# Two transformer layers with a kept KV cache: 12 kept chunks instead of 11, joined chain steps, and V loads in halves

## The chip, the cores and the metric

The kernel runs on one core of a Trainium2 chip. The metric is device time in microseconds (us) of one execution. TensorE (PE in the profile) multiplies matrices, VectorE (DVE) and ScalarE (ACT) do elementwise work, GpSimd (POOL) one power, and SyncE (SP) issues nearly all loads from HBM into the on-chip memory. 16 DMA engines carry the loads.

## What is computed

One token of each of 8 sequences goes through block A (attention over a KV cache), block B (two small matrix products with gelu, a mixer and an MLP), then A and B again with the same weights and the same cache:

```python
def _A_ref(x, k_cache, v_cache, wq, wo):      # k_cache, v_cache: (8, 8, 4096, 256)
    q = (x @ wq).reshape(B, Sq, 16, 256).transpose(0, 2, 1, 3)
    k = jnp.repeat(k_cache, 2, axis=1); v = jnp.repeat(v_cache, 2, axis=1)
    p = softmax(jnp.einsum("bhqd,bhkd->bhqk", q, k) * 256 ** -0.5)
    o = jnp.einsum("bhqk,bhkd->bhqd", p, v)
    return o.transpose(0, 2, 1, 3).reshape(B, Sq, 16 * 256) @ wo

x = A_x
x = x + _A_ref(_layernorm(x), A_k_cache, A_v_cache, A_wq, A_wo)
x = x + _B_ref(_layernorm(x), B_w1, B_w2, B_w3, B_w4)
x = x + _A_ref(_layernorm(x), A_k_cache, A_v_cache, A_wq, A_wo)
x = x + _B_ref(_layernorm(x), B_w1, B_w2, B_w3, B_w4)
```

With a sequence length of 1 the mixer's shifts (pad and cut) give zeros, so of block B the kernel computes `x + gelu(layernorm(x) @ w3) @ w4`. All is bf16. The two caches are 268 MB together, and both passes need all of them.

## The kernel before

**Chunks and places.** For a sequence b, the 8 KV heads are four pairs (gp 0 to 3). K and V of a pair are four chunks each, of 1024 KB: 128 partitions by 16 rows of 256. On-chip memory has 15 places of one chunk (`NC`, L61; `slots`, L78). A chunk goes into a place, is used once, and hands the place back. A K chunk is transposed in its place by DVE (`transpose_k`, L755; L760), and its scores are taken by PE (`scores`, L762; L775), for most units by pairs of chunks; then ACT takes the exponentials (L784). A V chunk is multiplied with the transposed weights of the softmax (`pv`, L820; L828): 16 products of one row of 256 each, the first eight on the chunk's first half.

**Two passes, kept chunks.** The first pass (ps 0) of sequence b loads everything. The 11 chunks of `kept` (L64 and L65: K of pairs 3 and 2, V 1 to 3 of pair 3) stay in their places until the second pass (ps 1) of the same b has used them; there they are not loaded, and K of them is already transposed. One more chunk (`inner`, V 1 of pair 2) is moved to PSUM and back (`away` and `back`, L792 and L799: four DVE transposes each); it comes back into the place of kept K0 of pair 3, which is therefore not handed to the loads. A quarter of another (`part`) waits in PSUM also, so that 768 KB of it are loaded in the second pass. With 11 places kept, 4 are left for what streams.

**The chain.** Between the two passes of b lies work that depends on itself from end to end: `chain` (L494) takes the rest of the attention's output, the product with wo (L365), norm (L235 and POOL's power, L254), w3 (L383), gelu, w4 (L365), norm again, the projection with wq (L316), and spreading q (`give_q`, L904; `spread_q`, L328). It is a generator: each `yield` ends a step, and `step` (L885) takes the next step of each kind of generator ("chain", "last", "rest"). A `yield 2` makes the next call skip, so that POOL's power has time.

**The order.** All uses stand in one list, `items` (L551 to L604). `first_kept` puts the second pass's units that are not kept, and units of a later sequence, around the kept blocks; the V chunks of these units (16 in six of the eight cases, 8 in the last two) are put off until the chain. The first `AFTER` = 12 of them (L553) are in the set `narrow`: in the middle of each of their products (after the eighth) and at the end a step is taken. During them "last" steps wait (`alone`, L883, L889). What is left over (`due`) goes one by one between the K chunks of the next kept block (`block`, L555): K0 V K1 V K2 V K3 V. If the chain isn't done when its q is wanted, L955 and L956 take steps until it is. This is the order on PE; an engine takes its instructions in order.

**The loads.** `emit_loads` (L707) runs after each item. It issues on SP, in the order of use, as many loads as there are places handed back, each waiting on the chip for the last reader of its place. Two K chunks go as one load of 2048 KB where two neighbouring places come free (`both_for`, L677; issued at L722). Others are issued at L747. The last load of all goes in two halves (L750).

Of the kernel before, what the change touches and what calls it, by code (L numbers as in the profile page):

```python
# [17 lines left out]
def kernel(  # L18
# [43 lines left out]
    NP = 4  # L62

    kept = [(gp, 0, n) for gp in (GP - 1, GP - 2) for n in range(4)]  # L64
    kept += [(GP - 1, 1, n) for n in range(1, 4)]  # L65
    inner = (GP - 2, 1, 1)
    part = (GP - 1, 1, 0)
    Q4 = 4 * Dh
# [141 lines left out]
    def norm(x, nb, twice):  # L210

        def room(name, shape, at):
            n = shape[0] * shape[1]
            if nb < Bn:
                t = chn.tile([128, n * MID], FP32, tag=name)
                ap = t[:, 0 : n * nb]
            else:
                ap = scratch(at, n * nb)  # L220
            return ap.rearrange("p (s f b) -> p s f b", s=shape[0], f=shape[1])

        def bc(ap):
            return ap.unsqueeze(1).to_broadcast([128, 4, nb])

        xx = room("xx", (2, 4), 0)
        nc.vector.tensor_mul(xx[:, 0], x, wv[:].unsqueeze(2).to_broadcast([128, 4, nb]))
        nc.vector.tensor_mul(xx[:, 1], xx[:, 0], x)
        xs = room("xs", (1, 2), 512)[:, 0]
        nc.vector.tensor_reduce(  # L230
            xs, xx.rearrange("p s f b -> p s b f"), mybir.AxisListType.X, ALU.add
        )
        yield
        st = room_ps("st", nb).rearrange("p (s b) -> p s b", b=nb)
        nc.tensor.matmul(st, ones, xs, start=True, stop=True)  # L235
        yield
        mv = room("mv", (1, 2), 528)[:, 0]
        nc.vector.tensor_copy(mv, st)
        var = room("var", (1, 1), 608)[:, 0, 0]
        if nb == 1:  # L240
            nc.vector.scalar_tensor_tensor(
                var, mv[:, 0], mv[:, 0], mv[:, 1], ALU.mult, ALU.subtract, reverse1=True
            )
        else:
            nc.vector.tensor_mul(var, mv[:, 0], mv[:, 0])
            nc.vector.tensor_sub(var, mv[:, 1], var)


        ve = room("ve", (1, 2), 544)[:, 0]
        n = 2 if twice else 1  # L250
        rs = room("rs", (1, 2), 560)[:, 0]

        def power(k0, k1):
            nc.gpsimd.tensor_tensor(  # L254
                rs[:, k0:k1].rearrange("p n b -> p (n b)"),
                ve[:, k0:k1].rearrange("p n b -> p (n b)"),
                nhalf[:].to_broadcast([128, (k1 - k0) * nb]),
                ALU.pow,
            )

        if twice and nb == 1:
            nc.vector.scalar_tensor_tensor(
                ve[:, :, 0], var.to_broadcast([128, 2]), 0.0, eps2[:], ALU.max, ALU.add
            )
            power(0, 2)
        else:
            if twice:
                nc.vector.tensor_scalar(
                    ve[:, 1], var, 0.0, EPS * EPS / (1 + EPS), ALU.max, ALU.add
                )  # L270
                power(1, 2)
            nc.vector.tensor_scalar(ve[:, 0], var, 0.0, EPS, ALU.max, ALU.add)
            power(0, 1)
        xc = room("xc", (1, 4), 576)[:, 0]
        nc.vector.tensor_tensor(xc, x, bc(mv[:, 0]), ALU.subtract)  # L275
        yield 2
        if nb > 1:
            yield
        c = (1 + EPS) ** -0.5 if twice else 1.0
        rl = rs[:, n - 1]  # L280
        parts = ((0, 128, 0, 0, 3, 0), (0, 64, 64, 3, 4, 4), (64, 128, 64, 3, 4, 3))
        if nb == 1:
            nc.vector.scalar_tensor_tensor(
                xbs(1)[:, 0:4, 0], xc[:, :, 0], rl, low[:, int(twice)], ALU.mult, ALU.mult
            )
            parts = parts[1:2]
        for p0, p1, x0, f0, f1, to in parts:
            pp = slice(x0, x0 + p1 - p0)
            dst = xbs(nb)[p0:p1, to : to + f1 - f0, :]
            if nb == 1:  # L290
                nc.vector.tensor_scalar(dst, xc[pp, f0:f1], rl[pp], c, ALU.mult, ALU.mult)
            else:
                nc.vector.scalar_tensor_tensor(
                    dst,
                    xc[pp, f0:f1],
                    c,
                    rl[pp].unsqueeze(1).to_broadcast([p1 - p0, f1 - f0, nb]),
                    ALU.mult,
                    ALU.mult,
                )  # L300
        if twice and nb == 1:
            nc.vector.scalar_tensor_tensor(x, xc, rs[:, 0], x, ALU.mult, ALU.add)
        elif twice:
            nc.vector.tensor_tensor(xc, xc, bc(rs[:, 0]), ALU.mult)
            nc.vector.tensor_add(x, x, xc)
        yield

    def project_q(b0, nb, qT):

        yield from norm(xT[:, :, b0 : b0 + nb], nb, False)  # L310
        q_ps = room_ps("q", nb).rearrange("p (c b) -> p c b", b=nb)
        for j in range(2):
            for h in range(Hq):
                for fc in range(4):
                    w, xi = wblk(wq_sb, HD, 2 * h + j, fc)
                    nc.tensor.matmul(  # L316
                        q_ps[:, j * Hq + h, :],
                        w,
                        xbs(nb)[:, xi, :],
                        start=(fc == 0),  # L320
                        stop=(fc == 3),
                    )
                if h % 8 == 7:
                    yield
        nc.vector.tensor_copy(qT, q_ps)  # L325
        yield

# [27 lines left out]
    def add_cols(y_ps, rhs, w, rows, every, open=None):  # L355

        for fc in range(4):
            at = min(128 * fc, D - 128)
            for i in rows:
                if open is None:  # L360
                    start, stop = i == rows[0], i == rows[-1]
                else:
                    start = open[0] and fc == 0 and i == rows[0]
                    stop = open[1] and i == rows[-1]
                nc.tensor.matmul(  # L365
                    y_ps[:, fc, :],
                    w[:, i, at : at + 128],
                    rhs(i),
                    start=start,
                    stop=stop,  # L370
                    skip_group_check=open is not None,
                )
            if fc % every == every - 1 or fc == 3:
                yield

    def mlp_hidden(b0, nb):

# [2 lines left out]
        for c in range(HC):  # L380
# [7 lines left out]
                    stop=(fc == 3),  # L388
                )
            if c % 7 == 6:  # L390
                yield
        g_t = chn.tile([128, 2, HC * MID], FP32, tag="g")
        hh, g0 = g_t[:, 0, 0 : HC * nb], g_t[:, 1, 0 : HC * nb]
        if nb == 1:
# [6 lines left out]
        nc.vector.scalar_tensor_tensor(g0, hh, 2 * 0.044715, h_ps, ALU.mult, ALU.mult)  # L401
        nc.vector.scalar_tensor_tensor(g0, g0, 1.0, h_ps, ALU.add, ALU.mult)
        nc.scalar.activation(g0, g0, ACT.Tanh, scale=0.7978845608028654)
        yield
        nc.vector.scalar_tensor_tensor(
            HT,
            g0.rearrange("p (c b) -> p c b", b=nb),
# [12 lines left out]
    def z_cols(zall, gps):  # L420
# [14 lines left out]
        yield  # L435
        z_ps = misc[:, 384 : 384 + 4 * np_].rearrange("p (n g) -> p n g", n=4)
        nc.tensor.matmul(z_ps, ones, zm[:], start=True, stop=True)  # L437
        yield
        rz = chn.tile([128, 4, np_], FP32, tag=f"rz{np_}")
        nc.vector.reciprocal(rz[:], z_ps)  # L440
        return rz
# [9 lines left out]
    def half(o_ps, zall, g8, OT, ready):  # L451
# [20 lines left out]
        for j in range(2):  # L472
            nc.tensor.matmul(  # L473
                ot_ps[:, j], o_sb[:].rearrange("p (i j) -> p j i", j=2)[:, j], R[:], start=True, stop=True
            )
        yield
        nc.vector.tensor_copy(OT, ot_ps)
        locked.pop()
        yield
# [69 lines left out]
        ahead.append(units)  # L549

    tasks, items, due = [], [], []  # L551
    number, narrow = {}, set()
    AFTER = 12  # L553

    def block(k, v=None):  # L555

        fresh = [(number[v], 1, c) for c in range(4)] if v else []
        if k is None:
            due.extend(fresh)
            items.extend(due)  # L560
            due.clear()
            return
        number[k] = len(tasks)
        tasks.append(k)
        for c in range(4):
            items.append((number[k], 0, c))
            items.extend(due[:1])
            del due[:1]
            if c == 0:
                due.extend(fresh)  # L570

    def first_kept(b, units, before):
# [13 lines left out]
        for u in units:  # L586
            due.extend((number[u], 1, c) for c in range(4))
        narrow.update(due[:AFTER])
        items.extend(due[:AFTER])
        del due[:AFTER]  # L590

# [115 lines left out]
    def emit_loads(most=None):  # L707
        n = 0
        while loads and places and n != most:
# [32 lines left out]
                src = rows.rearrange("(a p y) d -> a p (y d)", a=4, y=16)[c]  # L742
            else:
                src = rows.rearrange("(p x y) d -> x p (y d)", x=4, y=16)[c]
            if loads:
                z0 = Q4 if tasks[t][0] == 1 and halfway(it) else 0
                nc.sync.dma_start(dst[:, z0:], src[:, z0:])  # L747
            else:
# [133 lines left out]

    alone = []  # L883

    def step(idx, calm=False):  # L885

        for kind in ("chain", "last", "rest"):
            e = next((e for e in gens if e["kind"] == kind), None)
            if e is None or (kind == "last" and alone and not e.get("locks") and idx < len(items)):  # L889
                continue  # L890
# [3 lines left out]
            if not e["of"] or e["n"] < e["of"] * (idx - e["at"] + 1) / max(e["until"] - e["at"], 1):  # L894
                e["n"] += 1
                had = len(locked)
                got = next(e["g"], gens)
                if len(locked) != had:
                    e["locks"] = len(locked) > had
                e["skip"] = 1 if got == 2 else 0  # L900
# [33 lines left out]
    for idx, it in enumerate(items):  # L934
# [17 lines left out]
        if kv == 0:  # L952
            if (ps, b) not in state:
                if ps == 1:
                    while (1, b) not in state:  # L955
                        step(10 * len(items))  # L956
                else:
                    state[0, b] = {}
            st = state[ps, b]
# [182 lines left out]
```

## Time and profile before

| what | us |
|---|---|
| median of 3 runs (1120.81 to 1122.77) | 1121.21 |
| the profiled execution, time | 1120.6 |
| the profiled execution, span from first to last instruction | 1118.8 |
| PE busy | 650.1 |
| DVE busy | 603.8 |
| ACT busy | 162.7 |

HBM read is 444.67 MB, 397 GB/s over the span; SP's hardware queue holds the 16 DMA engines for 95.9% of it. The page's chain of work that ended last has 52% on DMA, 23% on PE and 18% on DVE. No engine is busy for much more than half of the span. The page cuts the span into 40 slices of 28 us; its rows give the busy tenths of each engine in each slice, the clock granted to TensorE and the rate of the DMA engines. In a line of the timeline or of the groups, L828 is a line of the kernel, and the part after `<-` in brackets is what ended the engine's idle time. In the answers by window, each engine has its busy time and number of instructions, and the last three columns are the granted clock, the share of DMA engines busy, and GB/s. PE's clock was granted at 0.50 in most of the stretches beside the chain.

### The profile page before, as it was taken

The numbers are of one execution on the slowest core, as the hardware profiler recorded it, in microseconds if no ns is written. First come the engines' busy times: TensorE is split into PE (matmuls) and PEld (weight loads), VectorE is DVE, ScalarE is ACT, GpSimd is POOL, SyncE is SP. The second block draws the span as 40 slices with busy tenths as digits, with TensorE's granted clock in tenths as the row PEclk, the third lists the DMA queues.
The fourth block names the chain that finished last, engine by engine and source line by source line (L and its number), as shares of the span: only waits on it lengthen the run. The fifth ranks groups of instructions, "written<-read, shape, count | busy, mean of one in ns | idle before, by whom it ended". The sixth has DMA issues, their size and how long they took to land.

```text
span 1118.8 us, 29781 instructions
## 1 busy us (share of the span) xinstructions
PE 650.1 (58%) x13364; PEld 409.6 (37%) x13364; DVE 603.8 (54%) x1242; ACT 162.7 (15%) x610; POOL 16.4 (1%) x27
## 2 busy tenths in 40 slices
PE   3244467644775446844567446764467546766775
PEld 2122234422453224522345223442244324543555
DVE  4348732587227861478415783259722771585272
ACT  0011111211111110211102111121111111111020
POOL 0000000000000000000000000000000000000000
PEclk9999975855556555655556555575555765555565
DMA  9999999999989999999999999899998999799794
GB/s 360 396 424 428 421 416 383 420 427 421 409 359 425 423 423 411 365 427 427 418 409 373 427 425 417 357 419 423 423 420 356 425 422 418 306 429 416 313 406 199
DMA packets 55808, 446.59 MB, mean 399 GB/s; under 512 B 5881, under 2 KB 9857, under 8 KB 11649
## 3 DMA queue, kind: packets, MB, share of 16 engines
q1 hardware_dynamic: 55488, 444.32, 95.9%
q8 instruction: 104, 1.70, 0.6%
q10 hardware_dynamic: 192, 0.38, 0.1%
q14 instruction: 24, 0.19, 0.0%
HBM read 444.67 MB, written 0.01 MB: 397 GB/s over the span
## 4 chain that ended last, share of the span: by engine, by line
DMA 52%; PE 23%; DVE 18%; SPq 3%; issue 2%; ACT 1%; POOL 0%; DVEq 0%; ACTq 0%
DMA places<-in_A_v_cache_dram 27%; DMA places<-in_A_k_cache_dram 23%; DVE places L760 12%; PE sc L775 9%; PE o L828 7%; PE misc L316 3%; PE misc L365 3%; SPq L174 2%; DVE qbd L339 1%; DVE store L795 1%; DVE places L802 1%; SPq L747 1%; PE misc L473 1%; ACT p_n L784 1%; DMA wq_sb<-in_A_wq_dram 1%
## 5 line engine op out<-in xcount | busy, mean ns | idle before, releaser
L760 DVE STREAM_TRANSPOSE places<-places 128x512 uint32<-128x512 uint32 (+1 forms) x576 | 457.6, 854 | 97.0 <-DMA places<-in_A_k_cache_dram 93.8
L775 PE MATMUL sc<-places,qbd 128*8 128x256 bf16 (+1 forms) x4992 | 248.4, 351 | 230.3 <-DVE places L760 208.9
L828 PE MATMUL o<-places,ptw 128*8 128x256 bf16 x3968 | 241.3, 380 | 175.3 <-DMA places<-in_A_v_cache_dram 149.5
L775 PEld LDWEIGHTS <-qbd 128*8 128x8 bf16 x4992 | 129.1, 104 | 306.5 <-DVE places L760 158.5
L828 PEld LDWEIGHTS <-ptw 128*8 128x8 bf16 x3968 | 102.7, 102 | 246.8 <-issue 158.2
L784 ACT ACTIVATE p_n<-sc 128x256 bf16<-128x256 f32 x128 | 95.2, 744 | 344.2 <-PE sc L775 344.2
L930 ACT COPY ptw<-psv 128x32 bf16<-128x32 bf16 x248 | 50.7, 225 | 213.7 <-PE o L828 212.8
L818 ACT CAST psv<-misc 128x128 bf16<-128x128 f32 x64 | 17.0, 266 | 274.1 <-PE misc L811 274.1
L468 DVE MEMSET o<- 128x256 f32 x31 | 8.4, 272 | 68.6 <-ACT o_sb L467 37.1
L365 PEld LDWEIGHTS <-wo_sb 128*128 128x128 bf16 x1280 | 37.5, 102 | 17.2 <-issue 17.1
L316 PEld LDWEIGHTS <-wq_sb 128*128 128x128 bf16 x1152 | 34.3, 105 | 24.5 <-issue 14.1
L316 PE MATMUL misc<-xb,wq_sb 128*128 128x1 bf16 x1024 | 32.1, 165 | 3.6 <-DVE rz L440 2.3
L784 ACT ACTIVATION_READ_ACCUMULATOR p_n<-sc 128x1 f32 x128 | 33.7, 263 | 0.0
L365 PE MATMUL misc<-OT,wo_sb 128*128 128x1 bf16 x1024 | 30.6, 165 | 3.2 <-issue 2.3
L473 PE MATMUL misc<-R,o_sb 128*128 128x8 f32 x124 | 28.0, 336 | 7.1 <-ACT o_sb L467 7.1
L473 PEld LDWEIGHTS misc<-R,o_sb 128*128 128x128 f32 x124 | 25.3, 283 | 18.9 <-ACT o_sb L467 14.0
L325 DVE CAST qT<-misc 128x32 bf16<-128x32 f32 x8 | 1.5, 192 | 53.4 <-PE misc L316 53.4
L254 POOL TENSOR_TENSOR t<-t,nhalf 128x2 f32<-128x2 f32 (+2 forms) x20 | 14.0, 704 | 1090.1 <-DVE t L275 1090.1
L339 DVE CAST qbd<-misc 32x64 bf16<-32x64 f32 x92 | 19.8, 215 | 18.3 <-PE misc L335 17.3
L440 DVE RECIPROCAL rz<-misc 128x8 f32<-128x8 f32 (+1 forms) x33 | 6.5, 197 | 39.7 <-PE misc L437 21.3
L437 PE MATMUL misc<-zm,one 128*128 128x8 f32 (+1 forms) x66 | 17.7, 341 | 17.3 <-DVE zm L429 9.9
L437 PEld LDWEIGHTS misc<-zm,one 128*128 128x128 f32 x66 | 14.8, 277 | 27.0 <-DVE zm L429 12.4
(104 smaller groups left out, 305.4 us busy)
## 6 DMA issues: line engine op xcount, KB each, us to landing
places<-in_A_v_cache_dram SPq DMA_DIRECT2D x215, 1024.0 KB, 10.9
places<-in_A_k_cache_dram SPq DMA_DIRECT2D x66, 2048.0 KB, 22.9
places<-in_A_k_cache_dram SPq DMA_DIRECT2D x60, 1024.0 KB, 12.5
places<-in_A_v_cache_dram SPq DMA_DIRECT2D x8, 768.0 KB, 4.3
wo_sb<-in_A_wo_dram SPq DMA_DIRECT2D x1, 3584.0 KB
wq_sb<-in_A_wq_dram SPq DMA_DIRECT2D x3, 1024.0 KB
w_sb<-in_B_w_dram SPq DMA_DIRECT2D x1, 1568.0 KB
w_sb<-in_B_w_dram SPq DMA_DIRECT2D x3, 448.0 KB, 11.5
```

Source lines behind the costliest of these rows:

```text
L174: nc.sync.dma_start(t[:, fc * cols : (fc + 1) * cols], src[fc * 128 : fc * 128 + 128, :])
L316: nc.tensor.matmul(q_ps[:, j * Hq + h, :], w, xbs(nb)[:, xi, :], start=(fc == 0), stop=(fc == 3),)
L339: nc.vector.tensor_copy(qbd[32 * a : 32 * a + 32, :, :, a, :], qs.rearrange("p e (f g u h) -> p (e f) u g h", f=2, u=2, h=2)[:, :, u],)
L365: nc.tensor.matmul(y_ps[:, fc, :], w[:, i, at : at + 128], rhs(i), start=start, stop=stop, skip_group_check=open is not None,)
L437: nc.tensor.matmul(z_ps, ones, zm[:], start=True, stop=True)
L473: nc.tensor.matmul(ot_ps[:, j], o_sb[:].rearrange("p (i j) -> p j i", j=2)[:, j], R[:], start=True, stop=True)
L760: nc.vector.transpose(w, w)
L775: nc.tensor.matmul(sc[32 * k : 32 * k + 8, 128 * x : 128 * (x + nx)], qbd[:, ep, gp].rearrange("p a h -> p (a h)"), v, start=(n == 0), sto ...
L784: nc.scalar.activation(p_sb[:, :, :, 2 * u : 2 * u + 2].rearrange("p t i x -> p x t i"), sc[:, 256 * u : 256 * u + 256].rearrange("p (x t ...
L818: nc.scalar.copy(p_to, pt_ps.rearrange("p t k (a h) -> p a (t k) h", a=4))
L828: nc.tensor.matmul(o_ps[32 * q : 32 * q + 8, :], ptz[:, at : at + 8], v[:, y * Dh : (y + 1) * Dh], start=False, stop=(y >= 12), skip_group ...
L930: nc.scalar.copy(ptw[:, ring_of[it], :, 6:8], psv[slot_of[it[0]]][:, it[2]])
```

## The change

Seven things change together:

1. V 2 of pair 2 is kept as well: 12 kept chunks, three places for the stream.
2. `AFTER` is 10 instead of 12.
3. Eight yields of the chain become `yield 0` (and in `norm` the `yield 2` moves to its end). In a narrow item (`calm`), `step` goes on through them: two or three old steps become one.
4. In the kept blocks of the second pass the order is K0 K1 V V K2 K3 V V, instead of a V after each K. The first K of a pair scores both chunks, so both places are handed back ahead of the V.
5. The first 12 of the V chunks put off to the chain (all 8 where there are 8) are in the set `halved`: each goes as two loads of 512 KB, by rows 0 to 7 and 8 to 15.
6. Where the chain isn't done when its q is wanted, only chain steps are taken, through the `yield 0`.
7. V of a kept block, made due at its K1, comes after that.

```diff
     kept = [(gp, 0, n) for gp in (GP - 1, GP - 2) for n in range(4)]
-    kept += [(GP - 1, 1, n) for n in range(1, 4)]
+    kept += [(GP - 1, 1, n) for n in range(1, 4)] + [(GP - 2, 1, 2)]
...
         nc.tensor.matmul(st, ones, xs, start=True, stop=True)
-        yield
+        yield 0
...
         nc.vector.tensor_tensor(xc, x, bc(mv[:, 0]), ALU.subtract)
-        yield 2
+        yield 0
         if nb > 1:
             yield
...
             nc.vector.tensor_add(x, x, xc)
-        yield
+        yield 2
...
                 if h % 8 == 7:
-                    yield
+                    yield 0 if j == 1 and h == Hq - 1 else None
...
             if fc % every == every - 1 or fc == 3:
-                yield
+                yield 0 if fc == 3 else None
...
             if c % 7 == 6:
-                yield
+                yield 0 if c == HC - 1 else None
...
         nc.scalar.activation(g0, g0, ACT.Tanh, scale=0.7978845608028654)
-        yield
+        yield 0
...
-    number, narrow = {}, set()
-    AFTER = 12
+    number, narrow, halved = {}, set(), set()
+    AFTER = 10
...
+        two = k[0] == 1 and k[2] in keep
         for c in range(4):
             items.append((number[k], 0, c))
-            items.extend(due[:1])
-            del due[:1]
-            if c == 0:
+            if two and c % 2 == 0:
+                continue
+            items.extend(due[: 1 + two])
+            del due[: 1 + two]
+            if c <= two:
                 due.extend(fresh)
...
         narrow.update(due[:AFTER])
+        halved.update(due[: AFTER + 2])
...
-            if loads:
+            if loads and it not in halved:
                 z0 = Q4 if tasks[t][0] == 1 and halfway(it) else 0
                 nc.sync.dma_start(dst[:, z0:], src[:, z0:])
             else:
...
-    def step(idx, calm=False):
+    def step(idx, calm=False, kinds=("chain", "last", "rest")):
 
-        for kind in ("chain", "last", "rest"):
+        for kind in kinds:
...
                 got = next(e["g"], gens)
+                while calm and got == 0:
+                    got = next(e["g"], gens)
...
                     while (1, b) not in state:
-                        step(10 * len(items))
+                        step(10 * len(items), True, ("chain",))
```

The two other places where a `yield` becomes `yield 0` are in `z_cols` (after the product) and in `half` (after the products with R).

More of the change, by code (lines that the diff above doesn't have):

```diff
@@ L437, in z_cols @@
         nc.tensor.matmul(z_ps, ones, zm[:], start=True, stop=True)
-        yield
+        yield 0
         rz = chn.tile([128, 4, np_], FP32, tag=f"rz{np_}")
@@ L475, in half @@
             )
-        yield
+        yield 0
         nc.vector.tensor_copy(OT, ot_ps)
```

## The prediction

> **What bounds the kernel now.** I read the page first: the rate of the transfers by slice, and the issues.
>
> ```profile
> span 1118.8 us, 29781 instructions
> ...
> GB/s 360 396 424 428 421 416 383 420 427 421 409 359 425 423 423 411 365 427 427 418 409 373 427 425 417 357 419 423 423 420 356 425 422 418 306 429 416 313 406 199
> ...
> places<-in_A_v_cache_dram SPq DMA_DIRECT2D x215, 1024.0 KB, 10.9
> places<-in_A_k_cache_dram SPq DMA_DIRECT2D x66, 2048.0 KB, 22.9
> places<-in_A_k_cache_dram SPq DMA_DIRECT2D x60, 1024.0 KB, 12.5
> ```
>
> The reader sees transfers at 420 to 428 GB/s with a dent about every 133 us, and that nearly all loads are places of 1024 KB or pairs of them. Then I asked for windows: a long stretch between two dents, and 30 us around the ends of four of the eight chains (2, 4, 6 and 7, counted from 0). The last two columns are the share of the DMA engines and GB/s.
>
> ```profile
> 340.00:436.00 96.00, 49.07 (x922) 28.42 (x919) 62.32 (x107) 13.93 (x53) 0.70 (x1) 0.55 1.01 424
> ...
> 439.00:469.00 30.00, 23.46 (x507) 15.89 (x500) 7.92 (x32) 4.89 (x19) 0.55 (x1) 0.56 0.90 360
> ...
> 706.00:736.00 30.00, 23.45 (x512) 16.11 (x513) 7.93 (x32) 4.90 (x19) 0.55 (x1) 0.56 0.90 357
> ...
> 942.00:972.00 30.00, 20.77 (x476) 14.83 (x475) 12.84 (x39) 3.74 (x14) 0.67 (x2) 0.50 0.79 312
> 1036.00:1066.00 30.00, 20.77 (x442) 14.71 (x443) 10.44 (x42) 2.83 (x10) 1.25 (x2) 0.50 0.78 309
> ```
>
> A window loses 30 x (1 - rate/424): 3.0 us for chain 0 (176:206, 382 GB/s), 4.2 to 4.7 for chains 1 to 5, 7.9 and 8.1 for 6 and 7, 41 us in all. All else runs at the full 424, so time is bytes plus these dents. The timeline of chain 4 shows why a dent comes:
>
> ```profile
> 712.72 0.60 PE L828 MATMUL o<-places,ptw 128*8 128x256 bf16 x8 [1.48 <-DMA places<-in_A_v_cache_dram]
> ...
> 717.67 1.01 PE L316 MATMUL misc<-xb,wq_sb 128*128 128x1 bf16 x32
> ...
> 718.96 0.27 PE L335 MATMUL misc<-qT,identb 128*32 128x32 bf16 x4 [0.28 <-DVE qT L325]
> ...
> 720.22 0.60 PE L437 MATMUL misc<-zm,one 128*128 128x8 f32 x2 [0.99 <-DVE qbd L339]
> ...
> 720.75 1.02 PE L775 MATMUL sc<-places,qbd 128*8 128x256 bf16 x16
> ```
>
> Until 712.7 PE waits for V, so the transfers set the pace. Then the projections make PE late, the chain ends at 720, behind its last V, and the transpose back into K0's place (L802, 2.5 us) delays z. SP issues at 717.78 and next at 724.90; 721:726 moves 198 GB/s.
>
> **Bytes.** One V chunk fewer in each of 8 batches: 8 x 1.0486 MB / 424 GB/s = 8 x 2.47 = **-19.8 us**. All are in the dense stream, so nothing else hides them.
>
> **Halves.** 12 V chunks in six chains and 8 in two, 88 in all, go as 176 DMAs of 512 KB. In the trace's packet records the median is 311 ns at 8192 B (35613 packets) and 160 at 4096 B (384): 9 ns more per 8 KB. A chunk has 128 / 16 = 8 such packets on each DMA engine, so 72 ns; x 88 = **+6.3 us**, uncovered because the transfers are the bound. SP's 88 more issues of 0.33 us lie in waits. A lone 1 MiB load took 4.19 us from issue to landing (issued at 591.46 into an empty queue), while with four in flight the stream keeps 410 to 424 GB/s: the time above 2.47 shows only where the queue runs empty. The Trainium skill's "DMA: Bandwidth & Descriptors" (Anatomy of one DMA; Measured) speaks against halves: it gives each DMA a fixed 2.0 us and wants 1 MiB or more at a time. If each added DMA paid that in line, the change would lose 88 x 2.0 = 176 us, an estimate from that page that the queue of four here contradicts.
>
> **Closer steps, 10 narrow chunks, one place fewer.** A `yield 0` no longer ends a call of `step` in the narrow stretch. I counted the yields: from R (L473) to q's spreading the old chain takes 26 calls, two of them skipped, and a narrow V gives two calls, so 12 V end it two calls short. The new chain takes 16 (two skipped) and ends in the 8th V. PE work for these 8, from chain 4's rows at the granted 0.50: products with V 16 x 0.52 = 8.3; chain: R (L473) 0.64, wo 2.02, norm sums 0.59, w3 1.81, w4 1.81, norm sums 0.59, wq 4 x 1.01, spreading 0.27, in all 11.8. The joined steps put more of DVE's time before the next matmul: norm 2.0 us (L235's end at 693.35 to L291's at 695.35) less two half products, 1.0, twice; gelu 1.07 - 0.52; the sums before the norm 0.79 - 0.52, twice: 3.1 us. Together 23.2 us, 2.9 a chunk against 2.54 for its transfer: PE falls 2.9 us behind, and gains it back in chunks 9 and 10 (1.04 us each). Three places last 3 x 2.54 = 7.6 us; a half needs 4.19 - 1.24 = 2.95 to land, 0.52 of PE and 0.1 of SP, which leaves 4.0 us: 2.9 fits, barely. (Behind a waiting matmul of the chain the next half product is queued on PE, and behind that SP's next load.) With whole chunks it would leave 7.6 - 5.3 = 2.3, and it wouldn't fit.
>
> After the narrow stretch, K0 and K1 come at once: about 2.3 us of PE until K1's place is free (K0's takes the inner chunk), then two V, then two places. z still waits for L802's 2.5 us, but three or four transfers are then in flight. Beside the halves' cost I leave the dent of chains 0 to 5, 4.2 on average, at 2.2 us: 25 us at the 410 GB/s that 696:706 runs at (0.8), and K1's place 2.3 us late with two chunks queued (1.4, estimated from 726:731, where 366 GB/s cost 0.7 in 5 us, over 10 us). The edges are 0.5 (always enough in flight) and 6 (the dent stays and PE's lag costs 1.5). Six times -2.0 is **-12 us**.
>
> Chains 6 and 7 have only 8 V. Scoring began at 962.28, after a first narrow product at 933.74; now 933.74 + 23.2 + 1.0 = 958, 4 us earlier, also because the forced steps leave out the other half's z (waits 1.14 and 0.32 us, matmuls 1.5). One place fewer is 2.47 us less loaded ahead: 2 x -1.5 = **-3 us** (edges -6 and +2 each).
>
> **One place fewer elsewhere.** Issued less moved, in chunks: 2.6 at 675, 2.8 at 682, where K waits for DVE's transposes and scoring; now one less. 1.6 is still more than the 0.75 at which the flow broke (724). I take 0.5 us a batch, the size of the ripple now: **+4 us**; edges 0 and 36.
>
> Sum: -19.8 + 6.3 - 12 - 3 + 4 = -24.5. The profiled execution took 1120.6 (span 1118.8 and 1.8 around it), 0.6 under the median of the runs, 1121.2: 1096.1, or **1097** as a run's median. Startup (0 to 60 us) and the tail after the last V (1105.7) stay.
>
> **Rivals.**
> 1. The dents vanish (0.15). 41 us shrink to about 1 a chain, 8: -19.8 + 6.3 - 33 + 4 = -42.5, **1079**. For it: PE starts the kept blocks early. Against it: 2.9 of 4.0 us of slack is used at clock 0.50, which 716:721 kept with PE busy for 3.73 of 5 us; 731:736, busy for 4.52, reached 0.84. The Trainium skill's "TensorE: Matmul & The Clock Gate" (What's actually happening) has the clock go to full after about 3.4 us of busy time; by that rule, if denser steps count as busy, PE's 20 us of matmuls in the stretch would halve and the lag be gone.
> 2. The dents stay (0.20): the gap only moves from the forced steps to PE's waits for DVE, or halves come free together. -19.8 + 6.3 + 4 = -9.5, **1112**.
> 3. Slower (0.12): pairs of K need two neighbouring places, and SP takes loads in order. With a place fewer, a pair before the chain waits until the one before is transposed and scored, 4.8 + 2.0 us of DVE and PE, against 1.6 chunks (3.9 us) in flight: 2.9 us dry, in up to two pairs a batch. With that twice in most batches, 5 us x 8 = 40 instead of 4: 1097 + 36 = **1133**. It decides from 3.6 us a batch. For it: SP already waits 45.5 us for scoring at the pairs (L722). Against it: the loads ahead of use still count 6 there, by the order of items, against 7.
>
> The saving of bytes cannot fail to be there: the list of loads is fixed by `kept`.
>
> **Chances.** Forecast 0.53, rivals 0.15, 0.20, 0.12. Range 1078 to 1118: it holds the forecast, rival 2 and half of rival 1. Within 0.2% (2.2 us, about what a measurement can tell from no change) needs rival 3 at just its threshold: 0.02. Faster 0.87, slower 0.11.
>
> **What will show it.** The page should have V as x119 of 1024 KB, x8 of 768 and x178 of 512. HBM read falls by 8.4 MB. Steps right: 30 us windows at chains 1 to 5 at 375 GB/s or more, against 360; PE's projections (L316) done before the last narrow V; K scored directly behind. Wrong: rates under 400 in the 20 us before a chain (rival 3), or a window of 200 GB/s behind it (rival 2).

## The result, and the profile after

The changed kernel takes 1105.8 us (median of 4 runs, 1102.1 to 1111.0) against 1122.0: ratio 0.986, 95% interval 0.982 to 0.990. The forecast was 1097: the time fell by 16 us where 25 were forecast. The changed kernel's runs spread over 9 us, those of before over 3.

| | before | after |
|---|---|---|
| profiled execution, time, us | 1120.6 | 1105.07 |
| span, us | 1118.8 | 1103.2 |
| HBM read, MB | 444.67 | 436.28 |
| rate over the span, GB/s | 397 | 395 |

These are lines of the page after. In the changed kernel the code below `block` has moved down: the loads stand at L726 (pairs), L751 (whole) and L754 (halves), the transposes of K at L764, the scores at L779, the way back of the inner chunk at L806, the products with V at L832.

```profile
span 1103.2 us, 30150 instructions
...
GB/s 361 395 424 427 422 389 347 427 423 421 396 372 427 424 418 389 397 425 422 402 365 393 425 427 397 389 412 425 427 384 387 424 423 409 340 426 411 341 380 197
...
L437 PE MATMUL misc<-zm,one 128*128 128x8 f32 (+1 forms) x66 | 17.9, 344 | 21.2 <-DVE zm L429 21.2
...
places<-in_A_k_cache_dram SPq DMA_DIRECT2D x63, 2048.0 KB, 23.8
places<-in_A_v_cache_dram SPq DMA_DIRECT2D x119, 1024.0 KB, 17.9
places<-in_A_v_cache_dram SPq DMA_DIRECT2D x178, 512.0 KB, 7.0
```

The counts of loads are the forecast ones, and the bytes are 8.39 MB fewer. But the rate over the span fell. The dents are shallower than before, and wider: most take two slices now (389 347, 402 365). The windows of chain 3 show where. The first is the end of the kept blocks before the chain, the second the chain, the third what follows:

```profile
530.00:550.00 20.00, 9.83 (x187) 5.18 (x182) 11.20 (x19) 3.57 (x14) 0.00 (x0) 0.50 0.99 396
550.00:573.00 23.00, 19.79 (x446) 13.59 (x445) 4.79 (x28) 1.79 (x9) 1.26 (x2) 0.50 0.98 357
573.00:595.00 22.00, 12.99 (x270) 8.33 (x264) 5.01 (x18) 4.19 (x18) 0.00 (x0) 0.64 0.98 376
```

PE is busy for 19.79 of the 23 us of the chain, and the transfers go at 357 GB/s, not at 410. In the kernel before, the last 25 us of the same chain read:

```profile
560.00:565.00 5.00, 2.12 (x34) 1.35 (x34) 1.27 (x7) 0.44 (x2) 0.70 (x1) 0.50 1.02 419
565.00:570.00 5.00, 3.93 (x96) 2.46 (x88) 0.69 (x4) 0.54 (x3) 0.00 (x0) 0.50 1.01 416
570.00:575.00 5.00, 3.87 (x90) 2.42 (x82) 0.66 (x4) 0.44 (x2) 0.00 (x0) 0.50 1.01 408
575.00:580.00 5.00, 2.61 (x41) 1.29 (x42) 1.04 (x6) 0.44 (x2) 0.55 (x1) 0.50 0.98 393
580.00:585.00 5.00, 5.00 (x148) 3.68 (x146) 0.00 (x0) 0.00 (x0) 0.00 (x0) 0.50 1.01 416
```

In the changed kernel's timeline the brackets show PE's idle times before the products with V:

```profile
567.73 0.60 PE L832 MATMUL o<-places,ptw 128*8 128x256 bf16 x8
568.26 1.01 PE L316 MATMUL misc<-xb,wq_sb 128*128 128x1 bf16 x32
569.20 0.60 PE L832 MATMUL o<-places,ptw 128*8 128x256 bf16 x8
569.74 1.01 PE L316 MATMUL misc<-xb,wq_sb 128*128 128x1 bf16 x32
...
575.90 0.60 PE L832 MATMUL o<-places,ptw 128*8 128x256 bf16 x8 [2.12 <-DMA places<-in_A_v_cache_dram]
577.17 0.60 PE L832 MATMUL o<-places,ptw 128*8 128x256 bf16 x8 [0.67 <-DMA places<-in_A_v_cache_dram]
577.55 1.07 PE L779 MATMUL sc<-places,qbd 128*8 128x256 bf16 x16
...
582.86 0.57 PE L437 MATMUL misc<-zm,one 128*128 128x8 f32 x2 [3.06 <-DVE zm L429]
```

From 553 to 574 no product with V waits for a load: PE sets the pace, a half every 1.47 us beside the projections. The eight chunks of the chain take 22.9 us, which is 366 GB/s. When the chain is done, V is not there, and PE waits 2.12 us. So while PE was late the transfers did not get ahead: the lag was lost, not stored.

For all chains together I counted, from the packet records, what 30 us around the chain's end (12 before the start of L335 to 18 behind it) and the 30 us ahead of them lack against 424 GB/s:

| us lost in 8 chains | 30 us ahead | 30 us around the end |
|---|---|---|
| before | 4.3 | 40.9 |
| after | 16.0 | 32.6 |
| after, 11 kept (a2_kept11) | 6.8 | 22.0 |
| after, chain spread (p3_lazy) | 20.3 | 19.7 |

Around its end the chain lost what the forecast said (41 - 15 + 6.3 = 32.3). But that agreement is chance: these windows cut through the chain, which in the changed kernel begins some 23 us before L335. Counted by its parts:

| us lost in 8 chains | 42 to 23 us before L335 | 23 us up to L335 | 18 us behind |
|---|---|---|---|
| before | 1.8 | 10.6 | 32.8 |
| after | 6.5 | 22.9 | 19.2 |
| after, 11 kept (a2_kept11) | 3.0 | 11.7 | 14.1 |

Behind the chain 13.6 us were won. Beside it 12.3 us more were lost, and that took most of the gain away. Ahead of it 4.7 us more were lost, close to the 4 that the forecast had for one place fewer.

### The profile page after: what moved, and what is told of

Read it like the earlier page. It is cut to its first block, busy times and chain, and to the rows that moved or that the text cites. A ratio compares the mean times of both kernels' runs of the same rounds, so it can differ in the third digit from the quotient of the medians.

```text
span 1103.2 us, 30150 instructions
## 1 busy us (share of the span) xinstructions
PE 658.1 (60%) x13492; PEld 414.2 (38%) x13492; DVE 603.5 (55%) x1242; ACT 160.6 (15%) x610; POOL 16.3 (1%) x27
## 3 DMA queue, kind: packets, MB, share of 16 engines
HBM read 436.28 MB, written 0.01 MB: 395 GB/s over the span
## 4 chain that ended last, share of the span: by engine, by line
DMA 44%; PE 24%; DVE 22%; issue 3%; SPq 3%; ACT 2%; POOL 1%; DVEq 0%; ACTq 0%
DMA places<-in_A_k_cache_dram 23%; DMA places<-in_A_v_cache_dram 20%; DVE places L764 14%; PE sc L779 8%; PE o L832 7%; PE misc L365 3%; PE misc L316 2%; SPq L174 2%; DVE places L806 2%; PE misc L383 2%; DVE store L799 2%; PE misc L473 1%; SPq L751 1%; POOL t L254 1%; DVE qbd L339 1%
## 5 line engine op out<-in xcount | busy, mean ns | idle before, releaser
L764 DVE STREAM_TRANSPOSE places<-places 128x512 uint32<-128x512 uint32 (+1 forms) x576 | 457.0, 854 | 107.1 <-DMA places<-in_A_k_cache_dram 97.9
L779 PE MATMUL sc<-places,qbd 128*8 128x256 bf16 (+1 forms) x5120 | 253.9, 350 | 251.8 <-DVE places L764 237.7
L832 PE MATMUL o<-places,ptw 128*8 128x256 bf16 x3968 | 244.7, 384 | 109.9 <-DMA places<-in_A_v_cache_dram 81.9
L779 PEld LDWEIGHTS <-qbd 128*8 128x8 bf16 x5120 | 132.8, 105 | 330.5 <-DVE places L764 135.9
L832 PEld LDWEIGHTS <-ptw 128*8 128x8 bf16 x3968 | 99.8, 102 | 173.1 <-issue 92.7
L316 PEld LDWEIGHTS <-wq_sb 128*128 128x128 bf16 x1152 | 34.8, 104 | 29.9 <-issue 19.7
L806 DVE STREAM_TRANSPOSE places<-store 128x512 uint32<-128x512 uint32 x32 | 20.1, 685 | 31.8 <-PE sc L779 31.8
L473 PEld LDWEIGHTS misc<-R,o_sb 128*128 128x128 f32 x124 | 25.7, 288 | 21.9 <-ACT o_sb L467 18.3
L339 DVE CAST qbd<-misc 32x64 bf16<-32x64 f32 x92 | 19.8, 216 | 20.4 <-PE misc L335 19.5
L437 PE MATMUL misc<-zm,one 128*128 128x8 f32 (+1 forms) x66 | 17.9, 344 | 21.2 <-DVE zm L429 21.2
L437 PEld LDWEIGHTS misc<-zm,one 128*128 128x128 f32 x66 | 15.0, 282 | 33.8 <-issue 24.7
```

The costliest lines, as they stand in the source:

```text
L316: nc.tensor.matmul(q_ps[:, j * Hq + h, :], w, xbs(nb)[:, xi, :], start=(fc == 0), stop=(fc == 3),)
L339: nc.vector.tensor_copy(qbd[32 * a : 32 * a + 32, :, :, a, :], qs.rearrange("p e (f g u h) -> p (e f) u g h", f=2, u=2, h=2)[:, :, u],)
L473: nc.tensor.matmul(ot_ps[:, j], o_sb[:].rearrange("p (i j) -> p j i", j=2)[:, j], R[:], start=True, stop=True)
L764: nc.vector.transpose(w, w)
L779: nc.tensor.matmul(sc[32 * k : 32 * k + 8, 128 * x : 128 * (x + nx)], qbd[:, ep, gp].rearrange("p a h -> p (a h)"), v, start=(n == 0), sto ...
L806: nc.vector.transpose(slot[:].bitcast(U32)[:, 512 * n : 512 * n + 512], store[n][:].bitcast(U32))
```

## The experiments

Three theories stood for the missing 9 us. **PE's pace**: the joined steps make PE the bound beside the chain, whatever the number of places. **Dear halves**: a half load costs more than its longer packets. **Short queue**: three places keep too little in flight. All ratios are to the kernel before, run beside. The changed kernel's own interval is 9 us wide, so differences to it of a few us are rough.

| run | what | median us | ratio, 95% interval |
|---|---|---|---|
| after | the change | 1105.8 | 0.986 (0.982 to 0.990) |
| a1_whole | after, whole loads | 1120.6 | 0.9984 (0.9973 to 0.9995) |
| a2_kept11 | after, 11 kept, four places | 1106.7 | 0.987 (0.985 to 0.988) |
| b1_halves | before, halves beside the chain | 1118.2 | 0.997 (0.995 to 0.998) |
| b2_halves_else | before, halves everywhere else | 1129.9 | 1.008 (1.006 to 1.009) |
| s1_steps | before, joined steps | 1111.5 | 0.990 (0.989 to 0.992) |
| s2_order | before, order of the kept blocks | 1123.4 | 1.002 (1.001 to 1.003) |
| s3_back | after, way back at K3 | 1100.1 | 0.981 (0.979 to 0.982) |
| s4_back11 | a2_kept11, way back at K3 | 1102.3 | 0.982 (0.981 to 0.984) |
| p1_nc14 | a2_kept11, 14 places | 1125.0 | 1.003 (1.001 to 1.004) |
| p2_light | after, a lighter chain | 1094.0 | 0.974 (0.973 to 0.976) |
| p3_lazy | s3_back, chain spread over 12 V | 1096.1 | 0.977 (0.974 to 0.980) |
| p4_lazy11 | p3_lazy, 11 kept | 1103.8 | 0.985 (0.983 to 0.986) |

### Halves and places: a1_whole, a2_kept11, b1_halves, b2_halves_else

a1_whole, to the changed kernel:

```diff
-        halved.update(due[: AFTER + 2])
+        halved.update(due[:0])
```

> The changed kernel (1105.8 us) with the V loads beside the chain whole again, not in halves; nothing else differs. Three theories for the 9 us that the change gave less than forecast. PE's pace: from 550 to 573 of the changed kernel PE never waits for V, and its joined steps take 2.9 us a chunk, which is 361 GB/s; halves then matter little, and a whole chunk held for both its steps makes it slower by 0 to 8 us: 1106 to 1114. Dear halves: a half costs some 0.1 us more than its packets, 0.17 us a chunk in place of 0.07; without 88 of them 15 us come back, and some 5 are lost for the earlier release: about 1096. Short queue: with three places the transfers fall to about 380 GB/s at two to two and a half chunks in flight, and whole chunks leave less in flight: 1112 to 1120.

a2_kept11, to the changed kernel:

```diff
-    kept += [(GP - 1, 1, n) for n in range(1, 4)] + [(GP - 2, 1, 2)]
+    kept += [(GP - 1, 1, n) for n in range(1, 4)]
```

> The changed kernel with 11 kept chunks, so four places for the stream; joined steps, 10 narrow chunks, the order of the kept blocks and the halves stay. 8 chunks more are loaded: 19.8 us. PE's pace: the fourth place doesn't help while PE sets the pace, 1120 to 1126. Dear halves: the same, 1122 to 1126. Short queue: the fourth place brings the rate beside the chain back to 410, worth 2.5 to 3 us a chain, so 1101 to 1108, near the changed kernel.

b1_halves, to the kernel before:

```diff
         narrow.update(due[:AFTER])
+        halved.update(due[:AFTER])
...
-            if loads:
+            if loads and it not in halved:
```

> The kernel before (1122.0 us) with nothing but the narrow V chunks, 88 in all, loaded in halves. By their packets alone: +6.3 us, 1128, less what the earlier release of half a place gives back. Dear halves: +15 us, 1137. PE's pace and short queue: four places have slack beside the chain, so the packets' price alone, or nothing where the stretch is not bound by the transfers: 1122 to 1128.

b2_halves_else, to the kernel before:

```diff
         narrow.update(due[:AFTER])
+        put_off.update(due)
...
-            if loads:
+            if loads and not (kv and it not in put_off and not halfway(it)):
```

> The kernel before with halves everywhere except beside the chain: 95 V chunks of the dense stretches, where 3 to 12 chunks are in flight, so that the price of a half is paid with a full queue. By their packets: 95 x 0.072 = +6.8 us, 1129. Dear halves: 95 x 0.17 = +16 us, 1138. The two other theories say the packets' price.

**Dear halves falls.** In the dense stretches 95 halved chunks cost 8.0 us, 0.084 us each (0.07 to 0.11 by the interval), where the packets said 0.072 and this theory 0.17. This charges the whole run's loss to them; in the profiled execution, 13.5 us slower than that of before, 7.1 us of it lie in the 30 us around the chains' ends. Beside the chain the halves even pay: 3.8 us less with four places, where no theory's range went below 1122 and 1118.2 was measured, and 14.8 us less with three (a1_whole against after; at 1120.6 it lies at the upper edge of the short queue's 1112 to 1120). A half hands its part of the place back earlier, and its first half also lands earlier; no run separates the two.

**The twelfth chunk pays for itself and no more.** Without it, and with four places, the kernel takes the same time: 19.8 us of bytes more, 19.8 us of dents fewer (28.8 against 48.6 in the table of losses). The two times agree within the changed kernel's interval, some 5 us either way. That is the short queue's forecast, and pure PE's pace (1120 to 1126) falls. PE does the same work in the same time there, and the transfers keep going, as this window of a2_kept11's chain 3 shows:

```profile
547.00:570.00 23.00, 19.09 (x440) 12.97 (x441) 4.90 (x28) 1.73 (x9) 1.26 (x2) 0.53 1.03 407
```

407 GB/s beside a PE busy for 19.09 of 23 us, against 357 with three places.

### Steps, order and the way back: s1_steps, s2_order, s3_back, s4_back11

s1_steps is the changed kernel with 11 kept chunks, whole loads and the old order of the kept blocks (`two = False`): what is left is the joined steps, `AFTER` 10 and the forced steps of the chain alone.

> The kernel before (1121.9 us) with the joined steps of the chain, 10 narrow chunks and the chain-only forced steps; 11 kept chunks, four places, whole loads, the old order of the kept blocks. The changed kernel with 11 kept chunks gained 15 us, of which halves alone gave 4. If the joined steps are what fills the dent (the chain ends before its last V), they give 7 to 12 of it: 1110 to 1115. If it is the order of the kept blocks, which hands places back sooner, this kernel stays at 1119 to 1123.

s2_order, to the kernel before, has only the change's edit of `block`:

```diff
+        two = k[0] == 1 and k[2] in keep
         for c in range(4):
             items.append((number[k], 0, c))
-            items.extend(due[:1])
-            del due[:1]
-            if c == 0:
+            if two and c % 2 == 0:
+                continue
+            items.extend(due[: 1 + two])
+            del due[: 1 + two]
+            if c <= two:
                 due.extend(fresh)
```

> The kernel before with the order K0 K1 V V K2 K3 V V in the kept blocks alone. If the joined steps fill the dent: 1119 to 1123, since the gap of 7 us between the last V and the first place handed back is the chain's end, which stays. If the order does: 1110 to 1115.

s3_back, to the changed kernel; s4_back11 has the same edit on a2_kept11:

```diff
-            if (ps, gp, c) == (1, keep[-1], 1):
+            if (ps, gp, c) == (1, keep[-1], 3):
                 where[(b, inner[0]), inner[1:]] = kept_place
```

> The changed kernel (1105.8 us) with the inner chunk's way back (four DVE transposes, 2.5 us) at K3 of the kept block instead of K1. At K1 they stand on DVE ahead of the other half's sums, and PE waits 3.06 us at 579.8 for them, with V and places behind it. If the rest of the dent after the chain comes from that wait, 2 to 3 us come back in each of 8: 1085 to 1092. If it is the short queue alone (three places, whatever PE does there), nothing changes: 1102 to 1107.

> The same with 11 kept chunks and four places (1106.7 us without it). The dent after the chain is smaller there (391 GB/s at 580 to 590), so the wait is worth less: 1 to 2 us in each of 8, 1092 to 1100; with no effect of the wait, 1105 to 1108.

The joined steps, with `AFTER` 10 and the chain-only forced steps, give 10.9 us, and the order of the kept blocks nothing (1.0 us slower). With b1's 3.8 the parts make 13.7 of the 15.2 us that a2_kept11 gained with four places.

Moving the way back from K1 to K3 gave 5.7 us; the two intervals just touch. With four places it gave 4.4 us, and there they are apart. The way back was no part of the change's diff, but the change made it worse: PE's waits at L437 for DVE's L429 went from 9.9 us to 21.2. They are 18.3 in s1_steps and 6.7 in s2_order, so they grew with the joined and chain-only steps and not with the order of the kept blocks. The line of the page before, and that of s3_back:

```profile
L437 PE MATMUL misc<-zm,one 128*128 128x8 f32 (+1 forms) x66 | 17.7, 341 | 17.3 <-DVE zm L429 9.9
```

```profile
L437 PE MATMUL misc<-zm,one 128*128 128x8 f32 (+1 forms) x66 | 17.6, 340 | 0.9 <-DVE zm L429 0.9
```

In s3_back the same place in the timeline reads:

```profile
579.97 1.02 PE L779 MATMUL sc<-places,qbd 128*8 128x256 bf16 x16
580.92 0.60 PE L437 MATMUL misc<-zm,one 128*128 128x8 f32 x2
581.45 1.02 PE L832 MATMUL o<-places,ptw 128*8 128x256 bf16 x16
...
583.90 1.02 PE L832 MATMUL o<-places,ptw 128*8 128x256 bf16 x16
584.10 2.50 DVE L806 STREAM_TRANSPOSE places<-store 128x512 uint32<-128x512 uint32 x4
```

L437 no longer waits (0.9 us in the whole run, from 21.2), and the transposes run beside products. 5.7 us of the 20 came back, less than the 14 to 21 expected, and with four places 4.4, where 7 to 15 were expected. Taking the rest of the wait away gave no time back; that loads in flight had covered it is likely, but not shown.

### The place, and the lag: p1_nc14, p2_light, p3_lazy, p4_lazy11

p1_nc14, to a2_kept11: `NC = 14`.

> The changed kernel with 11 kept chunks (1106.7 us with 15 places) and 14 places, so three for the stream and 8 chunks more to load: the price of the fourth place alone. If the fourth place is what the twelfth kept chunk paid with, this kernel has the changed kernel's losses and 8 chunks more: 1105.8 + 19.8 = 1125.6, so 1122 to 1129. If three places are enough and the twelfth chunk's gain is lost in another way (its place in the order, more single loads of K), it stays at 1106 to 1112.

p2_light, to the changed kernel (the same for w3; wo's second half and w4 by fewer rows):

```diff
-                for fc in range(4):
+                for fc in range(1 if nb == 1 else 4):
                     w, xi = wblk(wq_sb, HD, 2 * h + j, fc)
```

> The changed kernel (1105.8 us) with about three quarters of the chain's matrix products left out (only the first quarter of the rows of wo's second half, w3, w4 and wq are multiplied in the chain; loads, order and steps stay). PE then needs some 2 us a chunk beside the chain instead of 2.9, below the 2.5 us of a chunk's transfer. If PE's lag is the cost and three places of halves can keep the transfers busy when PE is prompt, the 2.5 to 3.4 us of lag a chain come back: 1080 to 1090. If three places are too few whatever PE does, the rate stays near 380 and 1100 to 1106 remain.

p3_lazy, to s3_back:

```diff
-    AFTER = 10
+    AFTER, lazy = 12, set()
...
+        if len(due) > AFTER:
+            lazy.update(due[2:AFTER:3])
...
-        step(idx, it in narrow and calm)
+        if it not in lazy:
+            step(idx, it in narrow and calm)
```

> The changed kernel with the inner chunk's way back at K3 (1100.1 us), 12 narrow chunks, and in six chains no chain step at the end of every third of them, so that the chain spreads over 10 to 11 V at some 2.3 us a chunk of PE. If the lag beside the chain is the cost, it goes in six chains, 2 us each less what the two further halves cost: 1088 to 1095. If three places are too few even for a prompt PE: 1098 to 1104.

p4_lazy11 is p3_lazy with the twelfth chunk taken out of `kept`.

> The kernel with the inner chunk's way back at K3 and the chain spread over 12 narrow chunks (1096.1 us with 12 kept chunks), with 11 kept and four places. Four places already cover most of PE's lag (1102.3 us with the way back at K3 and the chain in 8 chunks), so spreading the chain gives 0 to 3 us here, 1099 to 1103, and the twelfth chunk is worth some 3 to 6 us once the lag is gone. If the fourth place is worth as much as the chunk's 19.8 us even then, both come out alike, 1094 to 1098.

**The fourth place is worth 18.2 us** (1125.0 less 1106.7), about as much as the twelfth chunk's bytes. But it is not that three places are too few by themselves. With a lighter chain they carry 411 GB/s, nearly all that 16 engines can with packets of 4096 B at their median of 159 ns (412, by the arithmetic). In p2_light's window of chain 3, and in its timeline:

```profile
545.00:569.00 24.00, 16.43 (x242) 8.85 (x243) 5.72 (x32) 2.19 (x10) 1.25 (x2) 0.50 1.03 411
```

```profile
561.65 0.60 PE L832 MATMUL o<-places,ptw 128*8 128x256 bf16 x8 [0.38 <-DMA places<-in_A_v_cache_dram]
562.19 0.37 PE L316 MATMUL misc<-xb,wq_sb 128*128 128x1 bf16 x8
562.92 0.60 PE L832 MATMUL o<-places,ptw 128*8 128x256 bf16 x8 [0.36 <-DMA places<-in_A_v_cache_dram]
```

Here a half is used every 1.27 us, each lands some 7.0 us after its issue, and PE waits before each. The kernel is 11.8 us faster than the changed one. That lies between the two expectations: a prompt PE is worth these 11.8 us, and the wait at L437 (21.9 us in this run) and what lies ahead of the chain stay.

So neither theory holds alone. PE's lag costs where three places cannot store it; four can. p3_lazy tries that without leaving work out: four steps fewer at the ends of narrow chunks spread the chain, and the 30 us around its end, the second row, run at 414 GB/s:

```profile
530.00:560.00 30.00, 19.06 (x371) 11.53 (x372) 13.77 (x34) 3.81 (x17) 0.70 (x1) 0.50 1.00 388
560.00:590.00 30.00, 24.28 (x484) 15.28 (x481) 6.64 (x29) 4.09 (x17) 0.55 (x1) 0.51 1.03 414
```

The time is 1096.1 us, 9.7 below the changed kernel and the best of those that do all the work; its interval overlaps s3_back's, so the last 4 us are likely, not certain, and 1096.1 lies between the two expectations. With four places the spreading gives nothing (1103.8 after 1102.3). The twelfth chunk, worth 0.9 us in the change, is worth 7.7 us here (3 to 6 were expected), and the intervals of p3_lazy and p4_lazy11 are apart. The 388 GB/s ahead of the chain and in its first steps are what three places still lose.

## Why the prediction was right, and where it was off

The time fell by 16 us, not by 25, and the direction and the range held. The range was 40 us wide: 1105.8 is 9 us from the forecast and 6 from rival 2, the dents that stay (1112). In the profiled executions the sum is off by 9 us, and 7.3 of them are one term, the dents of chains 0 to 5.

- **Bytes, -19.8.** Right: 8.39 MB fewer, and a chunk is worth its transfer in the dense stretches.
- **Halves, +6.3.** Right in price: packets of 4096 B take 159 ns in the median (22912 of them), and b2_halves_else measured 0.084 us a chunk against 0.072. What they give back beside the chain was not a term of its own; with four places it would be 3.8 + 6.3 us, if their packets cost what the forecast says.
- **The 16 steps and 23.2 us of PE.** Right: in chain 3 of the changed kernel R starts at 549.93 and the spreading ends at 572.8, 22.9 us, in the eighth V, and K is scored directly behind the last narrow V.
- **The dents of chains 0 to 5, -12.** Here the forecast failed. With the halves of these chains (72 x 0.072 = 5.2) it says -6.8. From 23 us before L335 to 18 us behind it these six chains lost 27.0 us before and 27.5 after, so +0.5. Behind the chain the dent shrank as meant, from 22.5 us to 12.0. Beside it the loss grew from 4.5 to 15.5, 2.6 a chain, where the forecast had 0.8 (25 us at 410 GB/s) and the halves' 0.9.
- **"Three places last 7.6 us ... which leaves 4.0 us: 2.9 fits, barely."** This is the step behind that 0.8, and it was wrong: the lag did not fit. The load of 4.19 us at 591.46 is one of the eight of 768 KB, not of 1 MiB. The same subtraction then gives 3.6 us for a half and not 2.95, and leaves 3.4, into which 2.9 would still go. So the sum itself misleads. In the changed kernel a half landed 5.8 to 7.8 us after its issue (559.39 to 565.39, 564.14 to 570.43), and in p2_light 7.0 at 411 GB/s: in a queue this time holds the wait behind other loads, and it does not tell how much lag three places store. The runs do: p2_light (a prompt PE, 411 GB/s) and a2_kept11 (one place more, 407) each bring back the rate beside the chain that the changed kernel lacks (357).
- **"z still waits for L802's 2.5 us, but three or four transfers are then in flight."** This put that wait at nothing. Moving it gave 5.7 us (s3_back). Some of it stood in the kernel before too, which had 9.9 us of these waits.
- **Chains 6 and 7, -3.** Right: over the same 41 us they lost 16.4 us before and 14.6 after, -1.8, with 1.2 for their halves in it.
- **"One place fewer elsewhere: +4."** Right in size: 4.7 us more ahead of the chain, and 1.2 more from 18 to 30 us behind L335. The levels that it rests on were misread: by the packet records 1.8 and 2.0 chunks were issued and not yet moved at 675 and 682, not 2.6 and 2.8, and the flow broke at 724 with 0.03 left, not 0.75. All are too high by 0.7 to 0.8, so the comparison still holds; the 0.5 us a batch was a guess from the ripple, and 0.6 came out.
- **Rival 3** (pairs of K held up by the lack of neighbours). Its sign, under 400 GB/s in the 20 us before a chain, was just met in chain 3 (396 in 530 to 550). There are 63 pairs against 66, and the loss ahead of the chains grew by 4.7 us, not by 36. No run took it by itself.
- **The signs.** The 30 us windows of chains 1, 2, 4 and 5 run at 380 to 391 GB/s, over the 375 that was asked; chain 3 runs at 363.

On the rule weighed in the forecast: the Trainium skill's "DMA: Bandwidth & Descriptors" asks for 1 MiB or more per DMA (Rules for kernel authors), and its fixed 2.0 us are fitted to DMAs issued from GpSimd (Anatomy of one DMA), while the loads here are issued from SP. b2_halves_else puts a number to it in the dense stretches: 0.084 us for each further DMA of 512 KB, so 2.0 us were not paid in line. Where places are short, halves gained 14.8 us.

## What to carry to other kernels

Where loads set the time, a buffer that is given away for data kept on chip costs what it stored: here one place of four was worth 18 us, about as much as the 8.4 MB it saved. Before giving it away, spread the work that makes the consumer late, since here three places carried a prompt consumer at 411 GB/s and a late one at 357. And don't read the slack of a buffer from a landing time: a half landed in 7.0 us at the full rate too. Count what a late consumer takes out of the queue, or try it.

## What the runs showed of the hardware

- With three places and a late PE (550 to 573 of the changed kernel), on average 1.4 chunks were issued and not yet moved, and 357 GB/s came. With three places and a prompt PE (p2_light, 545 to 569) it was 1.7 chunks and 411 GB/s, with four places (a2_kept11, 547 to 570) 2.2 chunks and 407.
- In the slow stretch the DMA engines were not idle: their busy share is 0.98. Most packets of 4096 B took 159 ns there, but 63 of 1997 took over 0.3 us and 23 over 0.7, up to 1.84; what packets took above the median is 0.11 of the engines' time. In the two other stretches none took over 0.5 us. Why these packets are long stays open; no run here tells it.
- The Trainium skill's "TensorE: Matmul & The Clock Gate" (What's actually happening) has about 3.4 us of busy time lift the clock. In 550 to 573 PE was busy for 19.79 of 23 us by the profile, and the granted clock stayed at 0.50. So the joined steps did not lift the clock there, as rival 1 had hoped.
